# A planned attention and feed-forward kernel: TensorE's order is made to count changes between row-tiled and whole-array work, and the first phase gets its own banks and buffers

## The chip, the core and the metric

The kernel runs on one core of a Trainium2 chip. A core has TensorE (PE in the profile; PEld is its loading of weights), VectorE (DVE), ScalarE (ACT), GpSimd (POOL) and SyncE (SP), which here only issues the data transfers (DMA). The engines run their own instruction streams in order and wait for each other by semaphores. The metric is the device time of one execution in microseconds (us), as the median of several.

## The reference

Four batches of 12608 tokens with 128 channels go through two attentions with 32 inducing rows, and then through a feed-forward layer of width 1024 with a SoLU activation and a normalization. `mab(I, x)` is called p1 here, `mab(x, h)` is p2.

```python
def mab(q, kv):
    s = scale * (q @ kv.transpose(0, 2, 1))
    s = s - s.max(-1, keepdims=True)
    a = np.exp(s)
    a /= a.sum(-1, keepdims=True) + 1e-09
    return a @ kv
h = mab(I, x)
attn = mab(x, h)
...
h = x @ w_in                      # x is attn, as 50432 rows
h_max = np.max(h, axis=-1, keepdims=True)
e = np.exp(h - h_max)
sm = e / (np.sum(e, axis=-1, keepdims=True) + 1e-09)
solu = h * sm
mu = np.mean(solu, axis=-1, keepdims=True)
var = np.mean((solu - mu) ** 2, axis=-1, keepdims=True)
ln = (solu - mu) / np.sqrt(var + 1e-06) * g_ln
return (ln @ w_out).astype(np.float32)
```

The weights come as 64-bit floats and are rounded to 32 bits on the chip.

## The kernel before

A batch has 99 token tiles of 128 rows (396 tiles in all). Its work falls into parts, each written as a generator whose steps (`Op`) name an engine, a cost and what they wait for:

- `p1(b, k)`, nine groups a batch, 12 tiles each (the last has 3 less and a half): x is loaded (line 357), turned by TensorE in three pieces of four transposes (line 561), copied by ScalarE (547), stored to DRAM as xT (571); scores against the inducing rows (589); VectorE takes the maximum (605), TensorE spreads it over the partitions (`fold`, 614), ScalarE exponentiates (637, 639), VectorE turns the weights (659), TensorE gathers (665), VectorE accumulates (681).
- `combine(b)`: the sums and the pooled rows of the batch are brought together (707, 712, 714, the copy of h 716) and multiplied by w_in (726), so that a tile's hidden row is its 32 attention weights times `hs` (copies in 728).
- `p2(b, j)`: xT is read back (753), scores (768), softmax on VectorE, GpSimd and ScalarE (775 to 794), the weights turned by TensorE (804) and copied (812) to `aT`.
- `main` and `soft`, one tile at a time: h = aT times hs (902, products of 32 rows, four of which fit beside each other in the array), VectorE's negative scaling with the minimum (940), ScalarE's exponential (950), GpSimd's product (954), ScalarE's square (965), VectorE's transpose (978).
- `products`, for each four tiles two streams (op0 and op1, each two of the array's four row quarters): 32 steps with w_out (1023), evacuated (1045), finished in `finish` and stored.
- `weights_in`, `weights_out`: load (405), rounding on VectorE (410 to 419), ScalarE (421) and GpSimd (424, 426, 431); for w_out the gains (453), the column means by TensorE (464) and VectorE (469), and 16 transfers that spread it into `wc` (481).

All of this is put in order when the program is built. `Planner` keeps a clock for each engine. At each turn it takes the engine whose next step can begin first, and of that engine's steps that are ready within `SLACK` the one with the lowest priority number. `AFTER` is the time that it reckons between the end of a step on one engine and the start of what depends on it on another. Steps with an `alt` go to whichever engine is free. Where TensorE would stand idle for over `FILL` ns it issues transposes of the identity without use (fillers, line 488). `starts` says at which tile a p1 group, a `combine` or a p2 group is taken up (`P1_FROM`, `P1_STEP`, `P2_START`), `PRIO_P1` and `PRIO_P2` how urgent it is. What the chip does is then this fixed order, with the real waits.

"Row-tiled work" is lines 902 and 1023: matrices of 32 rows, in "beats" of four matmuls that lie side by side and that the profile records as two steps of four. "Whole-array work" is all else on TensorE. In the plan before, a step of whole-array work carries `SWITCH` (170 ns) in its own cost, whatever stands ahead of it.

Batch 0's p1 is the early phase. It borrows space that the later work uses: x goes into parts of `spare` and one of the `xn` buffers (six in all), the weights into the other `xn`; the PSUM banks are those of `op0` and `op1`, and two of a pool that makes room for `h`. `handover` and `handover_op` give them over. w_in is loaded behind the first x.

Of the kernel before, what the change touches and what calls it, by code (L numbers as in the profile page):

```python
# [11 lines left out]
U32 = mybir.dt.uint32  # L12
# [19 lines left out]
EAGER = 60  # L32
SWITCH = 170


def cut(total, most, unit):
# [20 lines left out]
LATE = -13  # L57
ON_EARLY = 3
P1_FROM = 0
P1_GO = 20  # L60
P1_STEP = 8
P2_AHEAD = 29
P2_START = 29
PR_EX = -2
# [5 lines left out]
PR_SQ = 1.5  # L70
PR_TU = 3
# [4 lines left out]
WOUT = -13.5  # L76

AFTER = {
    "PE": {"PE": 0, "ACT": 197, "DVE": 196, "POOL": 200, "SP": 250},
    "ACT": {"PE": 205, "ACT": 143, "DVE": 142, "POOL": 61, "SP": 50},  # L80
    "DVE": {"PE": 256, "ACT": 128, "DVE": 127, "POOL": 155, "SP": 50},
    "POOL": {"PE": 205, "ACT": 75, "DVE": 74, "POOL": 100, "SP": 50},
    "SP": {"PE": 1036, "ACT": 1000, "DVE": 920, "POOL": 1000, "SP": 1000},
# [15 lines left out]
class Op:  # L99
    def __init__(self, eng, cost, fn, *after, prio=None, alt=None, moves=0):  # L100
        self.eng, self.cost, self.fn, self.after, self.prio, self.alt, self.moves = eng, cost, fn, after, prio, alt, moves

# [16 lines left out]
class Planner:  # L119


    def __init__(self, slack):
        self.clock = dict(BEGIN)
        self.ops, self.blocked, self.seq, self.slack = [], 0, 0, slack
        self.window, self.busy, self.slow = 0, {}, True
        self.fill, self.scratch, self.data, self.now = None, (), 0.0, 0.0

# [83 lines left out]

    def run(self):
        clock = self.clock
        while self.ops:
# [3 lines left out]
            pick = min(  # L218
                (o for o in self.ops if o[0].eng == eng and o[1] <= limit),
                key=lambda o: (o[2][1] if o[0].prio is None else o[0].prio, o[3]),  # L220
            )
# [7 lines left out]
            end = start + (self._pe(start, op.cost) if eng == "PE" else op.cost)  # L229
# [9 lines left out]
def set_attention_then_solu_kernel(ctx: ExitStack, tc: tile.TileContext, x, inducing, w_in, w_out, g_ln, out):  # L239
# [51 lines left out]
    op_b = [buf([P, 2, 512], f"op{w}", where=psum) for w in range(2)]  # L291
    op_e = [o[:, i, :] for o in op_b for i in range(2)]
    early_h = tc.tile_pool(name="h_early", bufs=1, space=PSUM, side="right")
    where = early_h.__enter__()
    h_e = [buf([P, 512], f"h_e{i}", where=where) for i in range(2)]
# [16 lines left out]
    OS = Lock(bufs(2, [P, GS, C], "os"))  # L312
# [83 lines left out]
    w_in_ready = Event()  # L396
# [42 lines left out]
    def weights_in():  # L439
        g = yield from rounded(w_in_sb, w_in.bitcast(U32), conv, None, conv_free, -18.5)  # L440
        plan.set(w_in_ready, g)

    def weights_out():
# [11 lines left out]
        o = yield Op("POOL", 200, lambda: nc.gpsimd.memset(wc[:, :, C : C + 1], 1.0))  # L455
        for k in range(KC):
            d = yield Op("ACT", 251, gain(k), g, gd, prio=LATE)
        o_end = [o]
        g = [d]
        mp, rel = yield TRB  # L460
# [13 lines left out]
        give(TRB, mp, d)  # L474
        rows = wc.rearrange("p (k q) d -> p k q d", q=4)
        spread = []
        for a in range(4):
            for q in range(4):
                c = yield dma(
                    M * FF * 4,  # L480
                    lambda: nc.sync.dma_start(rows[a * M : (a + 1) * M, :, q, :C], wg[q * M : (q + 1) * M]), d, issue=600, prio=LATE,
# [30 lines left out]
    EARLY_X = Lock([spare[:, i * each : (i + 1) * each].rearrange("p (s c) -> p s c", c=C) for i in range(SPARES * FF // each)] + xn_b[:1])  # L512
    EARLY_T = Lock([vt_all[:, i * each : (i + 1) * each].rearrange("p (s t) -> p s t", t=P) for i in range(3 * GS * FF // each)] + [xT_b])
    e2 = xn_b[1].rearrange("p s c -> p (s c)")
    EARLY_EW = Lock([(e2[:, i * 2 * PG * M : (i * 2 + 1) * PG * M], e2[:, (i * 2 + 1) * PG * M : (i + 1) * 2 * PG * M].rearrange("p (s m) -> p s m", m=M)) for i in range(2)] + [ew_b])
    EARLY_TR = Lock(op_e[:3])
    EARLY_PB = Lock([*h_e, pb_b, op_e[3]])
# [3 lines left out]
    def p1(b, k):  # L521
# [33 lines left out]
        for c0 in range(0, n, 4):  # L555
# [7 lines left out]
            d = yield Op("PE", SWITCH + 108.7 * (c1 - c0), turn4, [d for d, at in xd if at < c1], trel, prio=None if early else RUSH)  # L563
# [28 lines left out]

        d = yield Op("PE", SWITCH + n * 60, scores, ready, rel, ind_ready.after)

# [19 lines left out]
        d = yield Op("PE", SWITCH + 110, lambda: nc.tensor.matmul(mq, lhsT=fold2, rhs=v["mdiag"], start=True, stop=True), d)  # L614
# [609 lines left out]
```

## Time and profile before

| | us |
|---|---|
| median of 3 runs | 1287.85 (1287.36 to 1296.73) |
| the profiled execution | 1285.68 |
| its span, first to last instruction | 1283.9 |
| TensorE matmuls busy | 1246.2 (97%) |
| TensorE weight loads busy | 1120.8 (87%) |
| VectorE, ScalarE, GpSimd busy | 1140.8, 1140.1, 1104.2 (89, 89, 86%) |
| line 1023 (25600 records) | 1007.7 |
| line 902 (6336 records) | 442.8 |
| mean granted TensorE clock | 0.992 |

Busy times of one engine's groups overlap on TensorE, as matmuls are pipelined and up to four lie beside each other; 1007.7 and 442.8 can't be added. A busy share tells how much of the span has some instruction running, not how well the array is filled. The time by stretch gives the same for parts of the span, with the granted clock and the DMA engines' share; restricted to one line it counts that line's records, so it also tells how far the program is.

### The profile page before, as it was taken

Reading aid. Unit: us, or ns where it says so; the run is one execution under the profiler, and the core shown is the slowest. Engines: PE = TensorE matmul, PEld = TensorE weight load, DVE = VectorE, ACT = ScalarE, POOL = GpSimd, SP = SyncE. Lnnn points to the kernel's source line nnn. Section 1 sums busy time; section 2 is a strip of 40 time slices with the busy share of each in tenths; the row PEclk is TensorE's granted clock in tenths of the full one; section 3 lists DMA queues with packets and bytes.
Section 4 is the critical chain, followed back from the end, with each engine's and each line's share of the span. In section 5 each row is a group of like instructions: output and inputs, shape, how many; then the busy total and the mean of one; then the engine's idle time right before and its main releaser. Section 6 shows DMA issues by size and latency. Waiting matters only on the chain.

```text
span 1283.9 us, 75837 instructions
## 1 busy us (share of the span) xinstructions
PE 1246.2 (97%) x34221; PEld 1120.8 (87%) x34221; DVE 1140.8 (89%) x1825; ACT 1140.1 (89%) x2418; POOL 1104.2 (86%) x981
## 2 busy tenths in 40 slices
PE   8899999999999999999999999999999999999996
PEld 6689888889888888889888998888989999999996
DVE  5589989999898989999888999899999999999993
ACT  5489999999889989999789999989988999999993
POOL 2388988889889988988888997978889999999994
PEclk9999999999999999999899999999999999999998
DMA  9652333331232233332133134233021211111111
GB/s 361 188 164 70 111 103 94 93 111 43 77 117 60 78 102 119 103 109 74 28 102 94 43 103 138 91 101 102 21 82 54 58 55 53 54 38 43 29 29 41
DMA packets 118149, 113.46 MB, mean 88 GB/s; under 512 B 76577, under 2 KB 83777, under 8 KB 117697
## 3 DMA queue, kind: packets, MB, share of 16 engines
q1 hardware_dynamic: 117824, 108.62, 27.6%
q8 instruction: 267, 4.37, 1.4%
q14 instruction: 58, 0.47, 0.1%
HBM read 54.30 MB, written 52.18 MB: 83 GB/s over the span
## 4 chain that ended last, share of the span: by engine, by line
PE 70%; DVE 3%; ACT 2%; issue 1%; POOL 1%; POOLq 0%; DVEq 0%; ACTq 0%
PE op L1023 46%; PE h L902 15%; PE tr L561 2%; PE tr L804 2%; PE tr L768 1%; PE pb L665 1%; PE pb L589 1%; ACT sq L965 1%; DVE spare L940 1%; DVE vt L978 1%; ACT eu L950 1%; POOL eu L954 1%; PE pb L726 0%; DVE hn L940 0%; PE pb L614 0%
## 5 line engine op out<-in xcount | busy, mean ns | idle before, releaser
L1023 PE MATMUL op<-wc,vt 32*128 32x129 f32 x25600 | 1007.7, 275 | 12.5 <-issue 8.4
L1023 PEld LDWEIGHTS op<-wc,vt 32*128 32x128 f32 x25600 | 945.4, 185 | 54.3 <-issue 39.8
L902 PE MATMUL h<-hs,aT 32*128 32x128 f32 x6336 | 442.8, 277 | 3.2 <-DVE spare L940 1.2
L902 PEld LDWEIGHTS h<-hs,aT 32*128 32x128 f32 x6336 | 387.9, 187 | 32.1 <-DVE spare L940 6.2
L954 POOL TENSOR_TENSOR eu<-spare,eu 128x1024 f32<-128x1024 f32 x144 | 341.2, 2376 | 33.8 <-ACT eu L950 33.4
L954 POOL TENSOR_TENSOR eu<-hn,eu 128x1024 f32<-128x1024 f32 x140 | 331.8, 2376 | 25.1 <-ACT eu L950 24.3
L978 DVE STREAM_TRANSPOSE vt<-eu 128x1024 f32<-128x1024 f32 x284 | 349.2, 1233 | 1.1 <-POOL eu L954 0.9
L965 ACT ACTIVATE sq<-eu 128x1024 bf16<-128x1024 f32 x284 | 298.9, 1053 | 17.2 <-POOL eu L954 13.7
L940 DVE TENSOR_SCALAR_CACHE_REDUCE hn<-h,rn 128x1024 f32<-128x1024 f32 x198 | 252.1, 1273 | 38.8 <-PE h L902 30.6
L940 DVE TENSOR_SCALAR_CACHE_REDUCE spare<-h,rn 128x1024 f32<-128x1024 f32 x198 | 251.8, 1272 | 37.2 <-PE h L902 28.2
L950 ACT ACTIVATE eu<-hn,nm 128x1024 f32<-128x1024 f32 x140 | 160.3, 1145 | 19.9 <-DVE hn L940 19.0
L950 ACT ACTIVATE eu<-spare,nm 128x1024 f32<-128x1024 f32 x144 | 164.9, 1145 | 10.7 <-DVE spare L940 10.5
L954 POOL TENSOR_TENSOR spare<-hn,spare 128x1024 f32<-128x1024 f32 x58 | 137.5, 2374 | 15.6 <-ACT spare L950 15.5
L954 POOL TENSOR_TENSOR spare<-spare 128x1024 f32<-128x1024 f32 x54 | 128.0, 2373 | 16.9 <-ACT spare L950 16.4
L978 DVE STREAM_TRANSPOSE vt<-spare 128x1024 f32<-128x1024 f32 x112 | 138.2, 1235 | 0.0
L965 ACT ACTIVATE sq<-spare 128x1024 bf16<-128x1024 f32 x112 | 117.7, 1051 | 9.3 <-POOL spare L954 8.3
L1100 ACT ACTIVATE os<-spare,fin 128x128 f32<-128x128 f32 (+1 forms) x276 | 86.9, 391 | 1.5 <-POOL fin L1085 1.2
L950 ACT ACTIVATE spare<-hn,nm 128x1024 f32<-128x1024 f32 x58 | 66.4, 1145 | 6.7 <-DVE hn L940 6.4
L1045 DVE COPY spare<-op 128x258 f32<-128x258 f32 (+1 forms) x123 | 50.2, 416 | 24.6 <-PE op L1023 23.6
L950 ACT ACTIVATE spare<-spare,nm 128x1024 f32<-128x1024 f32 x54 | 61.9, 1146 | 6.5 <-DVE spare L940 6.5
L965 ACT ACTIVATION_READ_ACCUMULATOR sq<-eu 128x1 f32 x284 | 54.2, 191 | 0.0
L561 PE MATMUL tr<-ident,xn 128*128 128x128 f32 x297 | 48.8, 287 | 0.4 <-DMA xn<-in_x_dram 0.4
(180 smaller groups left out, 1028.0 us busy)
## 6 DMA issues: line engine op xcount, KB each, us to landing
out_dram<-os SPq DMA_DIRECT2D x96, 256.0 KB, 2.4
xT<-xd SPq DMA_DIRECT2D x27, 768.0 KB, 4.6
xn<-in_x_dram SPq DMA_DIRECT2D x22, 768.0 KB, 5.4
xd<-xT SPq DMA_DIRECT2D x21, 768.0 KB, 4.3
dl<-dd SPq DMA_DIRECT2D x396, 1.0 KB, 2.4
xd<-vt SPq DMA_DIRECT2D x7, 768.0 KB, 10.6
spare<-in_x_dram SPq DMA_DIRECT2D x5, 768.0 KB, 10.3
xT<-xd SPq DMA_DIRECT2D x5, 512.0 KB, 4.2
```

What stands on the lines that cost most here:

```text
L561: nc.tensor.transpose(out=tr[:, (s - c0) * P : (s - c0 + 1) * P], in_=xn[:, s, :], identity=ident)
L589: nc.tensor.matmul(sc[g * M : (g + 1) * M, : nn * M], lhsT=indT, rhs=xT[:, :nn, g * M : (g + 1) * M], start=True, stop=True)
L804: nc.tensor.transpose(out=tr[:h, (q - q0) * P : (q - q0 + 1) * P], in_=a4[:, q * P : q * P + h], identity=ident)
L902: nc.tensor.matmul(hp[:, cols], lhsT=aT[rows, i // 2, :], rhs=hs[rows, cols], start=True, stop=True)
L940: lambda: nc.vector.tensor_scalar(out=hn, in0=hp, scalar1=rn, scalar2=None, op0=ALU.mult, op1=ALU.min, accum_out=nm),
L950: "ACT", 1133, lambda: nc.scalar.activation(e, hn, AF.Exp, bias=nm, scale=-1.0, accum_out=G["S"][:, s : s + 1]), d, rel, srel,
L954: d = yield Op("POOL", 2330, lambda: nc.gpsimd.tensor_tensor(out=e, in0=hn, in1=e, op=ALU.mult), de, prio=t + PR_MU)
L965: "ACT", 1040, lambda: nc.scalar.activation(sq, e, AF.Square, scale=1.0 / 32.0, accum_out=G["qe"][:, s, 0:1]), d,
L978: lambda: nc.vector.transpose(out=G["vtb"][:, : n * FF].rearrange("p (j s t) -> p j s t", j=M, s=n)[:, :, s, :], in_=e.rearrange("p (a f) ...
L1023: nc.tensor.matmul(op[:rows, a - 2 * w, : C + 1], lhsT=vt[q, k, :], rhs=wc[q, k, :], start=(k == 0), stop=(k == JB - 1))
L1045: return lambda: eng(F["raw"][:rows, i0 : i0 + 2, :], op[:rows, :, : C + 1])
L1100: nc.scalar.activation(os[:rows, q, :], raw[:, q, :], AF.Copy, scale=y[:, i0 + q : i0 + q + 1])
```

## The change

The plan gets a state for TensorE: `rows` says whether the last step was row-tiled. A change from one to the other costs `SWITCH` (now 200 ns) at that place alone; the steps themselves no longer carry it. `_alike` restricts the choice: as long as row-tiled steps are ready, whole-array steps are held back until two of them (`SEVERAL`) are ready or one has waited 2 us (`PATIENCE`); once in whole-array work, TensorE goes on with it while any is ready. The release times in `AFTER` rise by 40 ns in most pairs, `EAGER` from 60 to 120. A p1 group is taken up every six tiles (`P1_STEP` 8 before), p2's urgency falls (`P2_AHEAD` 29 to 20), other priorities move a little.

In the early phase six PSUM banks of an own pool serve (three for transposes, three beside `pb` for scores), x has nine buffers (two in `wc`, five in `spare`, both `xn`), its weights lie in the `os` buffers. `h`, `op0` and `op1` are made after it. w_in is the first load. `wc` can only be written when the first two groups are done, so its ones (line 455) and the 16 transfers wait for that; the mean uses a bank of the early scores and stands later.

```diff
-EAGER = 60
-SWITCH = 170
+EAGER = 120
+SWITCH = 200
+PATIENCE = 2000
+SEVERAL = 2
...
-LATE = -13
-ON_EARLY = 3
+LATE = -15
...
-P1_STEP = 8
-P2_AHEAD = 29
+P1_STEP = 6
+P2_AHEAD = 20
-PR_EX = -2
+PR_EX = -4
-PR_SQ = 1.5
-PR_TU = 3
+PR_SQ = 2
+PR_TU = 4
+WIN = -20.5
...
-    "PE": {"PE": 0, "ACT": 197, "DVE": 196, "POOL": 200, "SP": 250},
+    "PE": {"PE": 0, "ACT": 237, "DVE": 236, "POOL": 240, "SP": 290},
...
+    def _alike(self, able):
+        rows = [o for o in able if o[0].rows]
+        full = [o for o in able if not o[0].rows]
+        if not rows or not full:
+            return able
+        if not self.rows:
+            return full
+        late = self.clock["PE"] - min(o[1] for o in full) > PATIENCE
+        return full if late or len(full) >= SEVERAL else rows
...
+            able = [o for o in self.ops if o[0].eng == eng and o[1] <= limit]
+            if eng == "PE":
+                able = self._alike(able)
...
-            end = start + (self._pe(start, op.cost) if eng == "PE" else op.cost)
+            cost = op.cost
+            if eng == "PE" and op.rows != self.rows:
+                cost += SWITCH
+                self.rows = op.rows
+            end = start + (self._pe(start, cost) if eng == "PE" else cost)
...
-    op_b = [buf([P, 2, 512], f"op{w}", where=psum) for w in range(2)]
-    h_e = [buf([P, 512], f"h_e{i}", where=where) for i in range(2)]
+    bank_e = [buf([P, 512], f"bank_e{i}", where=where) for i in range(6)]
...
-        mp, rel = yield TRB
+        mp, rel = yield EARLY_PB
...
+        plan.set(centred, d)
+        for k in range(2):
+            yield p1_done[0][k]
+        o = yield Op("POOL", 200, lambda: nc.gpsimd.memset(wc[:, :, C : C + 1], 1.0), [d for e in p1_done[0][:2] for d in e.after])
...
-                    lambda: nc.sync.dma_start(..., wg[q * M : (q + 1) * M]), d, issue=600, prio=LATE,
+                    lambda: nc.sync.dma_start(..., wg[q * M : (q + 1) * M]), d, o, issue=600, prio=LATE,
...
-    EARLY_X = Lock([spare[...] for i in range(SPARES * FF // each)] + xn_b[:1])
+    EARLY_X = Lock([f[...] for f, n in ((wc_flat, 2), (spare, SPARES * FF // each)) for i in range(n)] + xn_b)
-    EARLY_TR = Lock(op_e[:3])
-    EARLY_PB = Lock([*h_e, pb_b, op_e[3]])
+    EARLY_TR = Lock(bank_e[:3])
+    EARLY_PB = Lock([*bank_e[3:], pb_b])
...
-            d = yield Op("PE", SWITCH + 108.7 * (c1 - c0), turn4, [d for d, at in xd if at < c1], trel, prio=None if early else RUSH)
+            d = yield Op("PE", 108.7 * (c1 - c0), turn4, [d for d, at in xd if at < c1], trel, prio=None if early else RUSH)
...
             op.fn = step
+            op.rows = True
...
-        early_h.__exit__(None, None, None)
-        give(H, buf([P, FF], "h", where=pool("h", 1, PSUM, side="right")), *done)
+        bank_pool.__exit__(None, None, None)
+        late = pool("late", 1, PSUM, side="right")
+        give(H, buf([P, FF], "h", where=late), *done)
+        for w in range(2):
+            give(OP[w], buf([P, 2, 512], f"op{w}", where=late), *done)
```

The order is the plan's result. Three places of it follow. First SP at the program's start, that is the transfers in the order in which they are issued (line 357 loads x, 405 a weight, 571 stores xT, 753 reads it back; in the new kernel 375, 423, 593, 775). Before:

```order
L357 DMA spare<-in_x_dram 128x512
L357 DMA spare<-in_x_dram 128x2x512
L498 DMA ind_sb<-in_inducing_dram 32x128
L357 DMA spare<-in_x_dram 128x3x512
L405 DMA eu<-in_moe_w_in_dram 128x2048
L357 DMA spare<-in_x_dram 128x3x512 x3
L357 DMA xn_70<-in_x_dram 128x3x512
L571 DMA xd<-vt 128x1536 x2
L357 DMA spare<-in_x_dram 128x3x512
L571 DMA xd<-vt 128x1536
L405 DMA eu<-in_moe_w_out_dram 128x8x256
L571 DMA xd<-vt 128x1536
```

And now:

```order
L423 DMA eu<-in_moe_w_in_dram 128x2048
L375 DMA wc<-in_x_dram 128x512
L519 DMA ind_sb<-in_inducing_dram 32x128
L375 DMA wc<-in_x_dram 128x2x512
L375 DMA wc<-in_x_dram 128x3x512
L375 DMA spare<-in_x_dram 128x3x512 x5
L375 DMA xn_70<-in_x_dram 128x2x512
L375 DMA xn_71<-in_x_dram 128x512
L375 DMA xn_71<-in_x_dram 128x256
L375 DMA xn_71<-in_x_dram 64x128
L593 DMA xd<-vt 128x1536
L423 DMA eu<-in_moe_w_out_dram 128x8x256
```

Six x loads stood ahead of the first store, and the last groups' loads behind stores and a weight; now w_in stands first, all of x behind it, and the stores behind x.

Next TensorE from the last gather of the early phase to the first tile (line 665 gather, 464 mean, 714 combine, 768 p2's scores, 726 hidden weights, 804 p2's transposes, 902 the tile's product, 488 fillers; in the new kernel 687, 480, 736, 790, 748, 826, 925, 509). Before:

```order
L665 MATMUL h_e_77<-spare,ew 32x128 x7
L464 MATMUL tr<-hn_83,ones_mean 128x128 x8
L714 MATMUL h_e_78<-fold,accn 128x128
L768 MATMUL op_73<-xT_87,h_0_123 32x128 x4
L726 MATMUL pb<-w_in_sb,h_0_123 128x512
L726 MATMUL op_72<-w_in_sb,h_0_123 128x512
L804 MATMUL op_73<-ident,a_94 128x128 x2
L902 MATMUL h<-hs_124,aT_95 128x128 x8
```

And now (729 is the sum of the weights, line 707 before):

```order
L729 MATMUL bank_e_76<-l_134,fold 128x1
L509 MATMUL tr<-ident 128x128 x11
L687 MATMUL bank_e_78<-xn_71,os_104 32x128 x7
L736 MATMUL bank_e_76<-fold,accn 128x128
L748 MATMUL bank_e_79<-w_in_sb,h_0_125 128x512
L748 MATMUL bank_e_80<-w_in_sb,h_0_125 128x512
L790 MATMUL tr<-xT_89,h_0_125 32x128 x4
L480 MATMUL pb<-hn_85,ones_mean 128x128 x8
L509 MATMUL pb<-ident 128x128 x14
L790 MATMUL tr<-xT_89,h_0_125 32x256 x4
L826 MATMUL tr<-ident,a_96 128x128 x2
L925 MATMUL h<-hs_126,aT_97 128x128 x8
```

The mean stood ahead of the combining product and now stands behind the hidden weights and p2's first scores; the hidden weights moved ahead of those scores.

Last TensorE near tile 140, beside p1 of batch 2 (lines as above; 561, now 583, are p1's transposes, 1023, now 1048, the products with w_out). Before:

```order
L1023 MATMUL op_73<-wc,vt 128x129 x2
L561 MATMUL tr<-ident,xn_70 128x128 x4
L1023 MATMUL op_72<-wc,vt 128x129 x2
L1023 MATMUL op_73<-wc,vt 128x129 x2
L1023 MATMUL op_72<-wc,vt 128x129 x2
L1023 MATMUL op_73<-wc,vt 128x129 x2
L1023 MATMUL op_72<-wc,vt 128x129 x2
L1023 MATMUL op_73<-wc,vt 128x129 x2
L665 MATMUL pb<-xn_71,ew 32x128 x12
L1023 MATMUL op_72<-wc,vt 128x129 x2
```

And now:

```order
L1048 MATMUL op_701<-wc,vt 128x129 x2
L1048 MATMUL op_702<-wc,vt 128x129 x2
L583 MATMUL tr<-ident,xn_70 128x128 x4
L687 MATMUL pb<-xn_71,ew 32x128 x12
L583 MATMUL tr<-ident,xn_70 128x128 x4
L925 MATMUL h<-hs_128,aT_99 128x128 x2
L1048 MATMUL op_702<-wc,vt 128x129 x2
```

Transposes and gather stood apart, each between products, and now stand together. Over the whole order whole-array work stands in 237 places between row-tiled work before and in 218 now (after the first tile), and there are 128 fillers before and 178 now.

## Rows read from the trace of the kernel before

**Rows 1.** the page's part 1: engine, busy us, share of the span, instructions.
```profile
PE 1246.2 (97%) x34221; PEld 1120.8 (87%) x34221; DVE 1140.8 (89%) x1825; ACT 1140.1 (89%) x2418; POOL 1104.2 (86%) x981
```

**Rows 2.** time by stretch: length, busy us by engine (records), clock, DMA share, GB/s.
```profile
8.00:40.00 32.00, 29.05 (x368) 20.51 (x369) 24.35 (x78) 19.78 (x45) 9.43 (x10) 1.00 1.02 399
193.00:251.30 58.30, 58.30 (x1590) 50.98 (x1590) 54.71 (x94) 55.04 (x120) 52.04 (x50) 1.00 0.32 102
1006.30:1206.30 200.00, 197.00 (x5862) 185.71 (x5862) 187.86 (x261) 190.04 (x394) 194.01 (x167) 1.00 0.17 45
```

**Rows 3.** time by stretch, line 902 alone (the product h): PE and PEld.
```profile
362.00:608.00 246.00, 87.71 (x1270) 77.39 (x1272) 1.00 0.30 94
610.50:670.80 60.30, 20.92 (x290) 18.35 (x290) 0.94 0.23 67
1006.30:1206.30 200.00, 81.14 (x1152) 69.90 (x1152) 1.00 0.17 45
```

**Rows 4.** time by stretch, line 665 alone (p1's gather).
```profile
362.00:608.00 246.00, 6.68 (x184) 4.53 (x184) 1.00 0.30 94
```

**Rows 5.** timeline of PE at seams: start, length, line, operation, tiles, count.
```profile
83.53 0.85 PE L768 MATMUL tr<-xT,h 128*32 128x384 f32 x8
84.31 0.38 PE L902 MATMUL h<-hs,aT 32*128 32x128 f32 x2
...
91.13 0.85 PE L589 MATMUL pb<-xT,indT 128*32 128x384 f32 x8
91.91 0.66 PE L561 MATMUL tr<-ident,xn 128*128 128x128 f32 x4
92.50 0.83 PE L1023 MATMUL op<-wc,vt 32*128 32x129 f32 x18
...
602.12 2.08 PE L1023 MATMUL op<-wc,vt 32*128 32x129 f32 x68
...
604.80 0.28 PE L902 MATMUL h<-hs,aT 32*128 32x128 f32 x2
605.00 0.64 PE L665 MATMUL pb<-xn,ew 128*32 128x128 f32 x16
605.58 2.29 PE L1023 MATMUL op<-wc,vt 32*128 32x129 f32 x72
```

**Rows 6.** timeline of PE before the first tile.
```profile
39.94 0.53 PE L561 MATMUL op<-ident,spare 128*128 128x128 f32 x3
...
49.10 2.05 PE L464 MATMUL tr<-hn,ones_mean 128*128 128x128 f32 x16
50.99 0.39 PE L714 MATMUL h_e<-fold,accn 128*128 128x128 f32 x2
...
53.09 1.13 PE L726 MATMUL pb<-w_in_sb,h 128*128 128x512 f32 x2
...
56.35 0.38 PE L902 MATMUL h<-hs,aT 32*128 32x128 f32 x2 [0.46 <-ACT aT L812]
```

**Rows 7.** timeline of SP: the issue of the last x loads.
```profile
26.72 2.20 SPq L357 DMA_DIRECT2D spare<-in_x_dram  x3
```

**Rows 8.** timeline of VectorE before the first tile.
```profile
51.26 1.22 DVE L469 TENSOR_TENSOR hn<-tr,hn 128x1024 f32<-128x1024 f32 x1 [1.37 <-PE tr L464]
```

**Rows 9.** timelines of GpSimd and ScalarE: w_out's conversion and gains.
```profile
39.07 2.51 POOL L424 TENSOR_TENSOR hn<-hn,eu 128x512 f32<-128x512 f32 x2 [1.00 <-ACT hn L421]
47.51 2.45 ACT L453 ACTIVATE hn<-hn,g_sb 128x128 f32<-128x128 f32 x8
```

**Rows 10.** timeline of PE at the end of batch 1: the wait for accn.
```profile
635.81 0.79 PE L714 MATMUL pb<-fold,accn 128*128 128x128 f32 x2 [1.92 <-DVE accn L712]
```

**Rows 11.** time by stretch, all engines, at the end of batch 1.
```profile
635.00:640.00 5.00, 4.19 (x66) 3.96 (x70) 3.31 (x5) 2.28 (x4) 2.36 (x2) 0.54 0.03 3
```

**Rows 12.** waits: engine, line, tile, releaser: us in all, times, longest.
```profile
PEld op L1023 <- issue: 39.8, 151, 1.8
PEld h L902 <- DVE spare L940: 6.2, 10, 0.8
```

More of the change, by code (lines that the diff above doesn't have):

```diff
@@ L290, in set_attention_then_solu_kernel @@
     xn_b = bufs(2, [P, PG, C], "xn")
-    op_b = [buf([P, 2, 512], f"op{w}", where=psum) for w in range(2)]
-    op_e = [o[:, i, :] for o in op_b for i in range(2)]
-    early_h = tc.tile_pool(name="h_early", bufs=1, space=PSUM, side="right")
-    where = early_h.__enter__()
-    h_e = [buf([P, 512], f"h_e{i}", where=where) for i in range(2)]
+    bank_pool = tc.tile_pool(name="early", bufs=1, space=PSUM, side="right")
+    where = bank_pool.__enter__()
+    bank_e = [buf([P, 512], f"bank_e{i}", where=where) for i in range(6)]
     tr_b = buf([P, 512], "tr", where=psum)
@@ L439, in weights_in @@
     def weights_in():
-        g = yield from rounded(w_in_sb, w_in.bitcast(U32), conv, None, conv_free, -18.5)
+        g = yield from rounded(w_in_sb, w_in.bitcast(U32), conv, None, conv_free, WIN)
         plan.set(w_in_ready, g)
@@ L591, in scores @@
                 )
-        d = yield Op("PE", SWITCH + n * 60, scores, ready, rel, ind_ready.after)
+        d = yield Op("PE", n * 60, scores, ready, rel, ind_ready.after)
         def free_xT():
@@ L613, in p1 @@
         )
-        d = yield Op("PE", SWITCH + 110, lambda: nc.tensor.matmul(mq, lhsT=fold2, rhs=v["mdiag"], start=True, stop=True), d)
+        d = yield Op("PE", 80 + 110, lambda: nc.tensor.matmul(mq, lhsT=fold2, rhs=v["mdiag"], start=True, stop=True), d)
         first = k == 0
@@ L743, in p2 @@
         A = aT_of[(b, j)]
-        bank = EARLY_TR if b == 0 and j < ON_EARLY else TRB
+        bank = TRB
         prev = []
@@ L1139, in set_attention_then_solu_kernel @@
                 starts.setdefault(NT * (b - 1) + int(P1_FROM + P1_STEP * k), []).append((p1(b, k), PRIO_P1(b, k)))
-        starts.setdefault(max(0, NT * (b - 1)), []).append((combine(b), PRIO_P1(b, NP - 1)))
+        starts.setdefault(max(0, NT * (b - 1)), []).append((combine(b), PRIO_P1(b, NP - 1) if b else -28))
         for j in range(len(at_groups[b])):
@@ L1166, in handover @@
         give(XT, xT_b, *done)
+        for o in os_b:
+            give(OS, o, *done)
         give(EW, ew_b, *done)
@@ L1169, in handover @@
             give(XN, a, *done)
-    def handover_op():
-        done = []
-        for k in range(NP):
-            d = yield p1_done[0][k]
-            done += d
-        for j in range(ON_EARLY):
-            d = yield aT_of[(0, j)]["all"]
-            done += d
-        for w in range(2):
-            give(OP[w], op_b[w], *done)
     def handover_tr():
```

54 lines of the change are left out of this document (29 added, 25 removed).

## The prediction

> **What bounds the kernel now.** I read the engines' totals first, then engine time by stretch, then the timeline wherever TensorE's order has a seam. TensorE's matmul row is busy 97% of 1283.9 us, its weight loads 87%, the other three engines 86 to 89% [rows 1]. A busy matmul row alone is no proof of a bound, so I go by pace. Line 902 leaves 16 records per token tile. From 362 to 608 us, with the next batch's first attention (p1) in the stream, 1270 records are 79.4 tiles in 246 us: 3.10 us a tile. From 1006.3 to 1206.3, with no p1 left, 1152 are 72 tiles in 200 us: 2.78 [rows 3]. The same 246 us hold 184 gather records (line 665), 24 to a full p1 group, so 7.7 groups [rows 4]. Each costs (3.10 - 2.78) x 79.4 / 7.7 = 3.3 us. On TensorE a group is three pieces of transposes at 0.66, scores 0.85, a gather of at least 0.64 and a fold like line 714's 0.39: some 3.9 us by the rows' lengths, of which each of the six pieces overlaps a little with what follows [rows 5, 6]. So p1 is paid nearly in full with TensorE time: beside p1, TensorE is the bound. In the last batch GpSimd is (194.0 of 200 us, against 190.0 on ScalarE and 187.9 on VectorE) [rows 2]; TensorE time saved there buys nothing.
>
> Three places lose more than this pace: the start, whose first tile comes at 56.35 us [rows 6]; the ends of the batches; and the seams where TensorE leaves its 32-row products.
>
> **The early phase.** The last x group sets it. Its transposes end at 40.47 us, since its loads are issued only at 26.72, when a buffer is free; then come fold and gather, the mean matmuls (line 464) from 49.10 to 51.15, the combining matmul (line 714) at 50.99, VectorE's line 469 (1.22 us, queued ahead of the copy of h), the first tile at 56.35 [rows 6 to 8]. The change issues all nine x loads with nothing but a 16 KB load between them, into nine buffers. From 8 to 40 us DMA ran at 399 GB/s [rows 2]; at that rate w_in and x (7.5 MB) are down in some 19 us, and TensorE no longer waits for x. It was busy 29.05 of those 32 us [rows 2], and 22 of the fillers (line 488) stand ahead of the last transposes, at 0.11 us a step: 3.0 + 2.4 = 5.4 us can go. The mean moves behind the hidden weights' matmuls (line 726). That takes some 1.2 us of VectorE (line 469) out of the chain and about 1 of TensorE, but the two line-726 matmuls, 1.13 each, now stand ahead of the first scores: nothing is won by it [rows 6, 8].
> What may hold the start instead is the weights' conversion: GpSimd begins on w_out at 39.07, ScalarE's gains end at 49.96 [rows 9], and in the new order the copies of hs stand behind these gains on ScalarE. The raw w_out can land earlier, with 9.3 MB ahead of and in it, about 23 us at the same rate, but VectorE takes it up between the same p1 groups as now. I take 5.5 us for the phase, between 0 (the gains end where they do) and 9 (TensorE loses all its fillers too).
> Costed at nothing: w_in first puts 1.05 MB, 2.6 us, ahead of the first x. The 32 warm-up transposes cover it; without them it costs those 2.6. The wc spread, 16 issues, follows as one block with the third xT load queued behind it on SP; that load's scores stand ahead of the fifth tile, and if it lands late, up to 3 us are lost (an estimate: one tile's pace; in the bounds).
>
> **The ends of batches.** Counted in TensorE's order, the combining matmul of the next batch stood after 93, 188 and 291 tiles; now it stands after 73, 177 and 276, the batches ending at 99, 198 and 297. The chain combine, hidden weights, p2, first tile gets 21 to 26 tiles of cover instead of 6 to 10. What it cost: at 633 us TensorE waits 1.92 us for accn (VectorE line 712), and the granted clock is 0.54 of 2.4 GHz over the stretch from 635 to 640, its lower level for nearly all of it [rows 10, 11]. Window 610.5 to 670.8: 290 records, 18.1 tiles, in 60.3 us [rows 3]. 18.1 x 2.78 is 50.3; lines 707, 714 and 726 take some 3.0 (0.39, as much again, and twice 1.13); that leaves 7.0, of which the end of a p1 group is at most 3.3. So 3.7 to 7.0 are lost here. I take 5 at this end and 1 for the other two, 6 in all, bounds 0 (the wait moves to tile 177 and stays) and 9.
>
> **Seams on TensorE.** Near 605 us the last pair of 32-row products starts at 604.80, a gather at 605.00, the products resume at 605.58 [rows 5]. A step of products is (2.08 - 0.28)/16 = 0.11 us, so without the gather the next would have begun at 604.91; the gather's own four steps are 0.44. Stopping and starting costs 0.67 - 0.44 = 0.23, and the first step behind it 0.1 more (18 steps in 2.29 us, 17 in 2.08): 0.33 us a round trip. The order has 218 trips instead of 237, and 21 fewer ahead of the last batch. But most merged pairs are of two kinds, a transpose with a gather, and between the kinds the array seems to stop again: scores take 0.78 us to the start of the transposes behind them (91.13 to 91.91), as much as alone to the next product (83.53 to 84.31) [rows 5]. Such a merge saves the entry and the slow step, 0.2. So between 19 x 0.2 = 3.8 and 21 x 0.33 = 6.9; I take 5, near the lower end. Against it, by a count of the order 21 more beats (two steps each, 0.22 us) run with half the array empty, 4.7 us; 4.1 of these lie in the last batch, where GpSimd sets the pace, so 0.6. The 50 additional fillers stand where the plan waits; were there no wait, they would cost 50 x 0.11 = 5.6 us.
>
> **Sum.** -5.5 - 6 - 5 + 0.6 = -15.9 us: the profiled execution, 1285.68 (span 1283.9), goes to 1269.8, and the median of the three runs, 2.2 us higher, to 1272.0.
>
> **Rivals.** (a) TensorE isn't the bound even beside p1, and the seams' time turns into waits: -5.5 - 6, or 1276. For it: ScalarE is busy 55.0 of 58.3 us in a stretch with p1 [rows 2]; against it, the 3.3 us a group. The Trainium skill (Perfetto Trace Analysis, Identifying the Most-Contended Engine) calls matmul busy time a poor measure and goes by the weight loads' share, here 87%; by that the seams give 0 and the time is this rival's.
> (b) The planner's release latencies rise by 40 ns, so instructions are put later where a wait was under-rated, and TensorE's waits for the other engines' buffers shrink. The largest group of these is 6.2 us [rows 12]; two such groups gone give 1259. Against it, far more idle (39.8 us) waits for nothing that the profile names [rows 12], and I see no edit that removes it.
> (c) Slower: p1 every six tiles instead of eight, in some 58 tiles of a batch instead of 87, crowds ScalarE and VectorE there and leaves TensorE idle behind it. If a group then costs 4.0 us while the rest still runs at 2.78, that is 0.7 x 27 = 19 us more: 1291. It cancels the gain from 3.3 + 15.9/27 = 3.9 us a group. For it: ScalarE at 55.0 of 58.3 beside p1 has 6% to give; against it, without p1 it is no less busy, 190.0 of 200 [rows 2], and the pace holds. The Trainium skill (Perfetto Trace Analysis, Optimization Strategy) speaks for this rival: regimes with different bounds gain from interleaving, which a shorter p1 undoes. No run so far shows it.
> (d) The rule hardly acts: seams and half-empty beats cancel, the conversion holds the start (-3), the ends give half (-3): 1282.
>
> **How the numbers follow.** Forecast 0.47, (a) 0.17, (b) 0.12, (c) 0.12, (d) 0.12. About 1% (12.9 us: below 1275, above 1300.7) is what a measurement of this kernel can tell from no change. The forecast, its own range 1264 to 1280, lies below 1275 in three cases of four (0.35), (b) nearly always (0.11), (a) in four of ten (0.07): faster 0.53. Slower takes the far part of (c), with the fillers' 5.6 us and the bounds of the start against me: 0.09. Same: 0.38. The range 1256 to 1289 leaves out the far half of (b), most of (c) and little else, 2 in 10.
>
> **What would show it.** The first tile near 51 us, with x landed by 24; if the gains end after 48, the conversion holds it. No clock dip and no wait for accn near the batches' ends. Some 218 stretches of whole-array work. A pace near 3.25 in the denser stretch and 2.78 behind it; a mean above 3.1 over a batch shows (c). TensorE's waits for VectorE and ScalarE near half: (b). A late third xT load, or pieces held back for a partner that new work waits for, would make the forecast wrong.

## The result and the profile after

The changed kernel takes 1302.05 us (median of 8 runs, 1297.66 to 1303.27) against 1288.22 for the kernel before (8 runs). The ratio is 1.0084, interval 1.0058 to 1.0109: it is slower by 0.6 to 1.1%, where 1272.0 was forecast, and it lies above the stated range (1256 to 1289). The profiled execution took 1297.66 us, its span is 1295.6, 11.7 us more than before's 1283.9.

The engines' totals and time by stretch (columns as in [rows 2]; the last three rows are those of line 925 alone, the old line 902, as in [rows 3]):

```profile
PE 1250.5 (97%) x34271; PEld 1129.3 (87%) x34271; DVE 1142.5 (88%) x1836; ACT 1136.5 (88%) x2410; POOL 1101.9 (85%) x981
```
```profile
8.00:40.00 32.00, 28.82 (x378) 21.13 (x379) 24.33 (x81) 20.21 (x49) 9.97 (x10) 1.00 1.04 400
393.00:398.00 5.00, 4.20 (x87) 4.20 (x90) 2.49 (x4) 4.39 (x11) 4.58 (x10) 0.66 0.08 11
635.00:640.00 5.00, 5.00 (x146) 4.68 (x142) 4.83 (x8) 4.59 (x13) 5.00 (x4) 1.00 0.36 109
1006.30:1206.30 200.00, 197.00 (x5798) 187.00 (x5802) 182.98 (x257) 183.64 (x385) 188.87 (x168) 1.00 0.17 46
...
362.00:608.00 246.00, 88.81 (x1248) 76.49 (x1248) 0.99 0.31 96
610.50:670.80 60.30, 20.91 (x304) 18.48 (x304) 1.00 0.19 48
1006.30:1206.30 200.00, 74.76 (x1082) 65.71 (x1084) 1.00 0.17 46
```

At the end of batch 1 the granted clock is 1.00 where it was 0.54 [rows 11]; a shorter dip now stands near the end of batch 0 (0.66 from 393 to 398 us). The window from 610.5 holds 304 records of h instead of 290. From 1006.3 to 1206.3 there are 1082 records instead of 1152 [rows 3]: the last batch, where the forecast expected nothing, is slower. TensorE is busy the same 197.00 us there, GpSimd 5 us less.

**A ledger of TensorE.** From the start times of all matmul records, between the first and the last 32-row product, I sorted the time by what TensorE was doing. "Trips" is whole-array work with entering and leaving it; "waits" is what a gap has beyond 0.25 us inside the products, 0.30 on entering and 0.34 on leaving:

```
us                        before    after   change   forecast
first tile                  56.4     57.0     +0.6    -5.5
32-row products            982.1    988.3     +6.2    +0.6 (half-empty beats)
trips (237, 218)           203.2    197.3     -5.9    -5.0
waits                       24.7     30.4     +5.7    -6 (ends of batches)
fillers behind tile 1        7.5     12.7     +5.2     0 (5.6 if no wait)
first to last product     1217.5   1228.8    +11.3
```

Next I cut the 31936 product records into 40 equal parts, and took parts 9 and 10, 19 and 20, 28 to 30 as the ends of the batches. The three middles with p1 in them took 722.4 us before and 754.9 after, the three ends 223.1 and 193.0, the stretch behind 139.3 and 138.0, the last eighth 132.8 and 143.0. So the ends gave back 30 us, as p1 and p2 were moved out of them, the middles took 32, and the last eighth lost 10: nearly the whole net loss of 11.3 is there.

Waits of TensorE that the profile names (columns as in [rows 12]), first one more of the kernel before, then after:

```profile
PEld h L902 <- DVE hn L940: 4.0, 7, 0.7
```
```profile
PEld op L1048 <- issue: 30.4, 100, 1.5
PEld h L925 <- DVE hn L965: 17.0, 38, 1.7
PEld h L925 <- DVE spare L965: 10.2, 22, 1.1
```

Idle time ahead of the products with w_out that nothing names fell from 39.8 us [rows 12] to 30.4, but h now waits 27.2 us instead of 10.2 for VectorE to take the h before it out of the one h buffer.

### The profile page after: what moved, and what is told of

It reads as the page before. It is cut to its first block, busy times and chain, and to the rows that moved or that the text cites. A ratio compares the mean times of both kernels' runs of the same rounds, so it can differ in the third digit from the quotient of the medians.

```text
span 1295.6 us, 75921 instructions
## 1 busy us (share of the span) xinstructions
PE 1250.5 (97%) x34271; PEld 1129.3 (87%) x34271; DVE 1142.5 (88%) x1836; ACT 1136.5 (88%) x2410; POOL 1101.9 (85%) x981
## 3 DMA queue, kind: packets, MB, share of 16 engines
q1 hardware_dynamic: 117824, 108.62, 27.2%
## 5 line engine op out<-in xcount | busy, mean ns | idle before, releaser
L1048 PEld LDWEIGHTS op<-wc,vt 32*128 32x128 f32 x25600 | 943.7, 185 | 54.0 <-issue 30.4
L1003 DVE STREAM_TRANSPOSE vt<-eu 128x1024 f32<-128x1024 f32 x284 | 350.3, 1236 | 22.8 <-POOL eu L979 21.9
L979 POOL TENSOR_TENSOR spare<-hn,spare 128x1024 f32<-128x1024 f32 x58 | 137.4, 2371 | 10.7 <-ACT spare L975 10.5
L1003 DVE STREAM_TRANSPOSE vt<-spare 128x1024 f32<-128x1024 f32 x112 | 138.2, 1236 | 9.3 <-POOL spare L979 8.9
L990 ACT ACTIVATE sq<-spare 128x1024 bf16<-128x1024 f32 x112 | 117.8, 1052 | 16.7 <-POOL spare L979 14.9
L1070 DVE COPY spare<-op 128x258 f32<-128x258 f32 x135 | 54.3, 415 | 16.3 <-PE op L1048 14.7
```

What stands on the lines that cost most here:

```text
L979: d = yield Op("POOL", 2330, lambda: nc.gpsimd.tensor_tensor(out=e, in0=hn, in1=e, op=ALU.mult), de, prio=t + PR_MU)
L990: "ACT", 1040, lambda: nc.scalar.activation(sq, e, AF.Square, scale=1.0 / 32.0, accum_out=G["qe"][:, s, 0:1]), d,
L1003: lambda: nc.vector.transpose(out=G["vtb"][:, : n * FF].rearrange("p (j s t) -> p j s t", j=M, s=n)[:, :, s, :], in_=e.rearrange("p (a f) ...
L1048: nc.tensor.matmul(op[:rows, a - 2 * w, : C + 1], lhsT=vt[q, k, :], rhs=wc[q, k, :], start=(k == 0), stop=(k == JB - 1))
L1070: return lambda: eng(F["raw"][:rows, i0 : i0 + 2, :], op[:rows, :, : C + 1])
```

## Experiments

Three counts are read from each kernel's TensorE order: trips to whole-array work behind the first tile, fillers there, and half-empty beats (what the products would take at 0.111 us a step, less what they would take with every step full). Before has 237, 59 and 56.5 us; after 218, 108 and 61.2. The planner is one list scheduler, so a change of any number re-deals the whole order; the counts say how.

### One part of the change taken back

```diff
-            if eng == "PE":
-                able = self._alike(able)
```


> After with the grouping rule off (the planner's choice of TensorE's next piece no longer looks at its mode; the charge of 200 ns for a change stays). Counted in the order: 250 round trips to whole-array work instead of 218, half-empty beats 60.1 us instead of 61.2, fillers behind the first tile 110 instead of 108. Theory T (TensorE is the bound over the whole program, and each trip, half-empty beat and filler in its order is paid): 32 x 0.3 - 1.1 + 0.2 = 8.7 us more than after's 1302.05, 1311. Theory W (the counts are hidden behind other engines, and the loss is of waits that the plan's new numbers make): no change, 1302, within 3.


Measured: 1312.77.

```diff
-EAGER = 120
+EAGER = 60
-    "PE": {"PE": 0, "ACT": 237, "DVE": 236, "POOL": 240, "SP": 290},
+    "PE": {"PE": 0, "ACT": 197, "DVE": 196, "POOL": 200, "SP": 250},
...
```


> After with the release latencies and EAGER of before (40 ns less each, 60 instead of 120). Counted in the order: 204 trips (14 fewer), half-empty beats 81.6 us (20.4 more), fillers behind the first tile 41 (67 fewer, 51 of them in the last tenth of the program). Theory T: 20.4 - 14 x 0.3 - 67 x 0.11 = 8.8 us more than 1302.05, 1311. Theory W: the loss of 10 us in the last eighth goes with the latencies that made the plan late there, 1292.


Measured: 1309.50; the last eighth of the products took 135.6 us instead of after's 143.0, with 0.4 us of waits instead of 5.6.

```diff
-P1_STEP = 6
-P2_AHEAD = 20
+P1_STEP = 8
+P2_AHEAD = 29
```


> After with P1_STEP 8 and P2_AHEAD 29 as before. Counted in the order: 226 trips (8 more), half-empty beats 82.4 us (21.2 more), fillers behind the first tile 200 (92 more, 58 of them in the last eighth). Theory T: 21.2 + 8 x 0.3 + 92 x 0.11 = 33.7 us more, 1336, or 1326 if the fillers lie in real waits. Theory W with the prediction's rival (c), that the dense p1 costs the middles of the batches some 10 us each: the middles come back to before's pace and the ends lose what they had won, 1292 to 1302.


Measured: 1329.73; middles 754.9 again, ends 218.2.

```diff
-PR_EX = -4
-PR_SQ = 2
-PR_TU = 4
+PR_EX = -2
+PR_SQ = 1.5
+PR_TU = 3
```


> After with the softmax's three order numbers of before (PR_EX -2, PR_SQ 1.5, PR_TU 3). Counted in the order: 216 trips, half-empty beats 81.6 us (20.4 more), fillers behind the first tile 125 (17 more). Theory T: 20.4 + 17 x 0.11 - 0.6 = 21.7 us more than 1302.05, 1324. Theory W: the new numbers put ScalarE's exponentials ahead and VectorE's transposes back, and these make GpSimd and the op products wait in the last eighth; without them 1292.


Measured: 1324.88.

All four are slower than after, and each lies within 3 us of theory T's number (for e3, inside its two). Theory W fails for the totals. Only its claim on the last eighth holds, in e2: there the waits went with the latencies and EAGER, but over the whole program 20 us of half-empty beats came in, and these are paid. The ledger of e2 shows it: products 1016.0 us instead of 988.3, waits 21.8 instead of 30.4. Trips cost what was forecast (0.33 us): e1's 32 more cost 11.9 us in the ledger, 0.37 each; after's 19 fewer saved 5.9, 0.31 each.

### Is TensorE the bound in the last batch?

The prediction costed half-empty beats at nothing there.

```diff
+                    if held is None:
...
+                    else:
+                        held.append((p["emit"], 2 * w, p["j"]))
...
+                held = [] if 306 <= t < 378 and t % 3 == 0 else None
-                beats(4, (1 - i % 2,), quarter)
+                beats(4, (1 - i % 2,), quarter, held)
+                for emit, a, k in held or ():
+                    emit(a, k)
+                    emit(a + 1, k)
```


> Before, with the same plan, but in 24 tiles of the last batch (every third from 306 on) the four pairs of h are issued together and the op pairs that went with them behind: both halves of the array are then used one after the other. By the order's count that is 12.3 us more of half-empty steps, all where GpSimd is busy 97%, and h itself is no later. Theory T (TensorE is the bound there too): 12 us over before, 1300. The prediction's step (GpSimd sets the pace there, so half-empty beats cost nothing): no change, 1288, within 3.


Measured: 1298.11, ratio 1.0089 (1.0064 to 1.0113), 10 us of the 12. Time by stretch, all engines, then h alone (line 905):

```profile
1006.30:1206.30 200.00, 196.82 (x5650) 186.31 (x5650) 181.52 (x252) 183.87 (x382) 187.94 (x163) 1.00 0.17 44
...
1006.30:1206.30 200.00, 76.44 (x1110) 67.07 (x1108) 1.00 0.17 44
```

GpSimd, 194.0 us in [rows 2], falls to 187.94 with the slower h (1152 records to 1110): it followed TensorE. Its 97% did not make it the bound: what is added to TensorE's order is paid, at the end too. The Trainium skill (Perfetto Trace Analysis, Identifying the Most-Contended Engine) does not judge TensorE by matmul busy time but by the share of its weight loads, and by its arithmetic against the peak. Over these 200 us that share is 93% in the kernel before (185.71 us, [rows 2]), below GpSimd's 97%, so it pointed away from TensorE; the measurement decides.

### Fillers, and EAGER

```diff
+    shown = []
...
-        nc.tensor.transpose(out=bank[:, :P], in_=ident, identity=ident)
+        shown.append(bank)
+        if len(shown) <= 127:
+            nc.tensor.transpose(out=bank[:, :P], in_=ident, identity=ident)
```


> After, with the same plan, but the 51 fillers that the plan put into the last eighth are not issued; the rest of the order is word for word that of after. If the plan's waits there are not real, each filler costs its 0.11 us: 5.4 us less than after's 1302.05, 1296.6. If they lie in real waits for other engines: no change, 1302, and the rows around their places show TensorE idle instead.


Measured: 1306.29, four more than after rather than five fewer. TensorE's timeline, with the fillers (after) and without:

```profile
1151.51 0.61 PE L925 MATMUL h<-hs,aT 32*128 32x128 f32 x8
1152.05 2.18 PE L509 MATMUL tr<-ident 128*128 128x128 f32 x18
1154.16 1.16 PE L925 MATMUL h<-hs,aT 32*128 32x128 f32 x16
```
```profile
1153.28 0.61 PE L929 MATMUL h<-hs,aT 32*128 32x128 f32 x8
1155.73 1.16 PE L929 MATMUL h<-hs,aT 32*128 32x128 f32 x16 [1.84 <-DVE hn L969]
```
Time by stretch around two of the places, after and then without fillers:
```profile
1140.00:1160.00 20.00, 19.84 (x546) 18.64 (x544) 17.64 (x27) 17.96 (x38) 18.94 (x19) 1.00 0.24 70
...
1260.00:1280.00 20.00, 18.82 (x621) 18.32 (x621) 15.29 (x20) 15.61 (x30) 15.73 (x13) 1.00 0.09 18
```
```profile
1140.00:1160.00 20.00, 18.01 (x480) 16.78 (x476) 17.00 (x26) 17.59 (x37) 18.52 (x20) 0.92 0.24 70
...
1260.00:1280.00 20.00, 17.35 (x425) 16.72 (x426) 16.48 (x23) 17.34 (x35) 17.05 (x11) 0.83 0.10 30
```
Where 2.18 us of fillers stood, TensorE waits 1.84 us for VectorE. The fillers lie in a real wait and cost nothing; without them the granted clock falls (0.92 and 0.83 instead of 1.00). That the 4 us are the clock's is likely, not shown. So the last eighth of after loses some 10 us to waits: 5.4 under fillers, 5.1 more of bare waits than before. At the place shown no op product stands in the wait, and h waits for its own buffer.

```diff
-EAGER = 60
+EAGER = 120
```


> Before with EAGER 120 instead of 60 alone: an op pair may join a beat that starts up to 120 ns, by the plan, ahead of its data. Counted in the order: half-empty beats 50.2 us instead of 56.5, 233 trips instead of 237, the same fillers. Theory T: 6.3 + 4 x 0.3 = 7.5 us less than before's 1288.22, 1281. If the pairs that join early make TensorE wait for VectorE's transposes or for the copies of op, what is won in beats goes there: 1288, with those waits (9.8 us in all at line 1023 for vt, and the copies at 9.9) risen by some 7 us.


Measured: 1289.72, ratio 1.0013 (0.9999 to 1.0027): no gain. The ledger has the products at 982.3 (982.1 before) and waits at 27.6 (24.7). So the beats that are full in the order saved nothing. That a pair joining before its data is there holds the beat is likely, not shown: the waits of TensorE's weight loads for vt and for VectorE's copies of op rose from 3.6 and 4.0 us to 5.7 and 7.2, less than the 7 us in all that were expected.

### Who makes the plan wait: the 40 ns

```diff
-    "PE": {"PE": 0, "ACT": 237, "DVE": 236, "POOL": 240, "SP": 290},
+    "PE": {"PE": 0, "ACT": 197, "DVE": 196, "POOL": 200, "SP": 250},
...
```


> After with the release latencies of before alone (40 ns less each); EAGER stays at 120. Counted in the order: 209 trips (9 fewer), half-empty beats 68.4 us (7.2 more), fillers behind the first tile 41 (67 fewer, none in the last eighth). If the 40 ns make the plan that waits in the last eighth, this eighth (143.0 us in after, 135.6 with both constants back) comes to some 135, and the whole to 1302 - 8 + 7.2 x 1.25 - 9 x 0.33 = 1300. If EAGER makes these waits, the eighth stays at 143 and the whole goes to 1308.


Measured: 1310.67, ten above the count. In the last eighth the waits fell from 5.6 us to 2.1 and the fillers went, so in after the 40 ns made most of the waits there; of the time lost there only half came back (138.2 us, where after has 143.0 and before 132.8). The excess is in the products (1018.9). Part of it goes with the granted clock, which is 0.50 to 0.63 between 70 and 80 us in the profiled execution: of the four executions, two had a mean clock of 0.985 and took 1314.3 and 1313.9 us, two had 0.993 and 0.990 and took 1305.0 and 1307.5. Why the counts miss the rest is open.

Now the 40 ns put into the kernel before, alone (e13), and EAGER alone taken back in after (e14):

> Before with the 40 ns longer release latencies alone (EAGER stays at 60). Counted in the order: 245 trips (8 more), half-empty beats 63.7 us (7.2 more), and 104 fillers in the last quarter where before has none. If the 40 ns alone make the plan wait there: the last quarter of the row products takes 272.1 + 104 x 0.11 = 283 us, and the whole comes to 1287.9 + 11 + 7.2 x 1.25 + 8 x 0.33 = 1311. If they do not, and EAGER 120 or the new order numbers did it in after: the quarter stays at 272 to 274, the whole at 1300.


Measured: 1329.82, ratio 1.0324 (1.0291 to 1.0357), 42 us. The last quarter took 292.6 us instead of 272.1; waits rose to 45.8 us, and not there alone:
```profile
PEld h L902 <- DVE hn L940: 12.0, 19, 1.3
PEld h L902 <- DVE spare L940: 11.3, 15, 1.8
...
PEld op L1023 <- DVE vt L978: 8.6, 19, 1.0
```


> After with EAGER 60 alone (the 40 ns stay). Counted in the order: 217 trips, half-empty beats 78.5 us (17.3 more), 136 fillers behind the first tile (28 more, 61 of them in the last eighth). If the 40 ns make the waits of the last eighth, it stays at 143 us or above, and the whole goes to 1302 + 17.3 x 1.25 = 1324. If EAGER made them, the eighth comes back to 136, and the whole to some 1316.


Measured: 1321.76, the last eighth 141.8. So EAGER 120 is not what slows the last eighth. The 40 ns were expected to spare TensorE waits (rival (b)) and did the opposite, in e13 and in after. How a longer latency in the plan leads to more waiting on the chip was not isolated.

### The other parts alone, on the kernel before

The edits are those of P1_STEP and P2_AHEAD above, and the rule with its charge, put into before.

> Before with P1_STEP 6 and P2_AHEAD 20 alone. Counted in the order: 245 trips (8 more), half-empty beats 66.5 us (10 more), the combining matmuls after 83, 180 and 279 tiles instead of 93, 188 and 291. By the counts: 10 x 1.25 + 8 x 0.33 = 15 us over before, less some 5 us at the end of batch 1 (the wait for accn of 1.92 us and the stretch at the low clock gone): 1298. By the prediction's rival (c) (a p1 group costs 4.0 us instead of 3.3 when p1 is dense, 27 groups) 19 us come on top: 1317. By the prediction's forecast (only the ends change): 1282.


Measured: 1312.91. The ends took 207.2 us instead of 223.1, the middles 760.5 instead of 722.4, so the steps pay 38 for 16. It is neither of the prediction's mechanisms: trips with their work cost 1.0 us more in all; the products took 16.7 more and waits 9.5. The wait for accn only moved: it was 1.92 us near 635 us, and is 1.32 near 319 and 1.43 near 952 here.

> Before with the grouping rule and its charge of 200 ns alone. Counted in the order: 212 trips (25 fewer), half-empty beats 83.0 us (26.5 more), fillers behind the first tile 9 (50 fewer). Theory T: 26.5 x 1.25 - 25 x 0.33 = 25 us over before's 1287.6, 1313 (1308 if the fillers' 5.5 us were paid). The prediction's step (trips saved are won, half-empty beats hardly cost): 25 x 0.33 = 8 us less, 1280.


Measured: 1310.48. Trips fell by 25 and saved 5.0 us in the ledger, the products took 32.6 more. Half-empty beats rose by 26.5 us in the order: held to groups of whole-array pieces, the planner paired fewer products, and that cost more than the trips saved. Within the change it is otherwise: e1, with the rule off, has 60.1 us of them where after has 61.2.

### The early phase

```diff
         hd = yield h_ready[b]
         (s2, mx, nr), srel = yield S2
+        if b == 0 and j:
+            yield aT_of[(0, 0)]["all"]
         sp, rel = yield bank
```


> After, but the attention groups behind the first of the first batch take their transposing bank only once the first group's weights are turned. The read is the first tile alone (the plan behind it comes out otherwise: 17 us more half-empty beats). If the first tile of after is late (56.97) because the second group holds the one bank while its load and its scores are outstanding, ahead of the first group's transposes, it comes at 52.5 to 53.5. If the weights' mean (2.05 us ahead of it) or the hs copies hold it, it stays at 56 to 57.


Measured: first tile 52.69 us (one execution; the whole kernel took 1311.02). TensorE's timeline, after and then this kernel:
```profile
31.23 0.99 PE L583 MATMUL bank_e<-ident,xn 128*128 128x128 f32 x7
...
46.47 0.49 PE L736 MATMUL bank_e<-fold,accn 128*128 128x128 f32 x2 [1.12 <-DVE accn L734]
...
49.67 2.05 PE L480 MATMUL pb<-hn,ones_mean 128*128 128x128 f32 x16
53.11 1.75 PE L509 MATMUL pb<-ident 128*128 128x128 f32 x14 [1.39 <-DVE hn L485]
54.79 0.64 PE L790 MATMUL tr<-xT,h 128*32 128x256 f32 x8
56.09 0.41 PE L826 MATMUL tr<-ident,a 128*128 128x128 f32 x2 [0.66 <-DVE s L797]
56.97 1.16 PE L925 MATMUL h<-hs,aT 32*128 32x128 f32 x16 [0.46 <-ACT aT L834]
```
```profile
49.79 2.05 PE L480 MATMUL pb<-hn,ones_mean 128*128 128x128 f32 x16
51.79 0.44 PE L828 MATMUL tr<-ident,a 128*128 128x128 f32 x2
52.69 1.16 PE L927 MATMUL h<-hs,aT 32*128 32x128 f32 x16 [0.46 <-ACT aT L836]
```
The last transposes of x end at 32.2 us instead of 40.5 [rows 6], and the combining matmul comes 4.5 us earlier. The other 3.8 us were lost behind x. VectorE's timeline in after:
```profile
34.67 1.18 DVE L433 SCALAR_TENSOR_TENSOR eu<-eu 128x1024 uint32<-128x1024 uint32 x1
35.89 1.23 DVE L434 SCALAR_TENSOR_TENSOR eu<-eu 128x1024 uint32<-128x1024 uint32 x1
...
37.89 0.42 DVE L627 TENSOR_REDUCE small<-pb 128x1 f32<-128x256 f32 x1
```
The scores that line 627 takes the maximum of were done at 31.3 us. VectorE comes to them at 37.89, behind the rounding of w_out (five instructions, lines 430 to 437, 4.5 us of the time from 32.72 on), and TensorE runs 26 fillers meanwhile. No run moves the rounding, so what it costs alone is not shown.

Then the first group's transposes, whose input is ready at 51.6, wait 4.5 us: the second group has taken the only transposing bank, and its load, the fillers ahead of it and its scores come first. Before, three groups had banks of their own.

The early phase with that wait, on the planner of before, with three values of EAGER (90 in e12, 60 in e15, 120 in e16):

> Before with the early phase of the change alone (nine x buffers, banks of its own, w_in first, output weights behind the first groups), with the wait that brought the first tile to 52.69 us, and EAGER 90. Counted in the order: 235 trips (2 fewer), half-empty beats 57.2 us (0.7 more), 38 fillers behind the first tile (21 fewer). If what the start wins stays won: 56.35 - 52.7 = 3.7 us less, 1284. If it is lost again behind the start (the early product groups wait for the output weights, or the plan's other order costs as much), 1288, and the time from the first tile to the tenth fortieth of the row products is 4 us longer than before's 326.8.


Measured: 1279.08, ratio 0.9922 (0.9900 to 0.9945), the fastest kernel of this study, and faster than both numbers expected.

> The early phase alone, as in the run before of that kind, but EAGER 60 as in before. Counted in the order: 237 trips, half-empty beats 66.1 us (8.9 more than with EAGER 90), 47 fillers (9 more). If the counts set the time: 1279.1 + 8.9 x 1.25 = 1290. If the gain of that run is the early phase's own: 1280.


Measured: 1288.59, ratio 1.0010 (0.9996 to 1.0024).

> The early phase alone with EAGER 120. Counted in the order: 238 trips (3 more), half-empty beats 54.2 us (3.0 fewer than with EAGER 90). If the counts set the time: 1279.1 - 3.0 x 1.25 + 1 = 1276. If what EAGER saves in beats goes into waits, as it did in before: 1279 to 1282.


Measured: 1293.11, ratio 1.0044 (1.0022 to 1.0066).

The first tile comes at 54.3, 54.0 and 53.9 us in the three, some 2.3 us ahead of before, and the ends differ by 14 us. So at most some 2 us of e12's gain is the early phase's, and with EAGER 60, as in before, nothing of that is left (e15). The rest is the plan that EAGER 90 happens to deal: waits of 18.7 us against 21.9 and 29.3, products 984.1 against 989.8 and 987.4.

### All kernels together

```
          trips  half-empty us  fillers  waits us  median us
before      237       56.5         59      24.7     1288.2
after       218       61.2        108      30.4     1302.1
e1          250       60.1        110      34.1     1312.8
e2          204       81.6         41      21.8     1309.5
e3          226       82.4        200      30.3     1329.7
e4          216       81.6        125      28.5     1324.9
e5          237       68.8         59      26.9     1298.1
e6          215       60.6         57      35.9     1306.3
e7          233       50.2         59      27.6     1289.7
e9          209       68.4         41      25.6     1310.7
e10         245       66.5         61      34.2     1312.9
e11         212       83.0          9      24.4     1310.5
e12         235       57.2         38      18.7     1279.1
e13         245       63.7        132      45.8     1329.8
e14         217       78.5        136      34.6     1321.8
e15         237       66.1         47      21.9     1288.6
e16         238       54.2         38      29.3     1293.1
```
A straight line through these 17 kernels, 1191 + 1.01 x half-empty + 1.62 x waits, leaves 4.2 us (root mean square) of a spread of 14.8. It is fitted, not a test, but these two quantities go with most of the spread. Waits can't be counted in the order; they need a run. The expectations that went by the counts came within 3 us in e1, e2, e4, e5, e11, e14 and e15; in e7, e9, e10, e13 and e16 the kernel was 9 to 19 us slower than they said.

**The parts do not add.** The rule, the steps and the 40 ns each make after slower when they are taken out of it, by 10.7, 27.7 and 8.6 us (e1, e3, e9). Put alone into before, the same three make that slower too, by 22.6, 25.1 and 41.8 us against its runs beside them (e11, e10, e13). So none of them has a price of its own; what one costs alone isn't what it costs within the change.

## Why the prediction was wrong, point by point

- **The bound.** "In the last batch GpSimd is; TensorE time saved there buys nothing" is the first step that failed. e5 shows that TensorE's order is paid there. A share of 97% was taken for a limit because TensorE's own 98.5% (197.00 of 200 us) was set aside. Two terms were put at next to nothing. The products, costed at 0.6 us more, took 6.2 more (4.7 by the count of half-empty beats). The 50 additional fillers, costed at nothing because the plan waits there, mark waits that are real and paid: with the bare waits beside them some 10 us, all in the last eighth.
- **The early phase.** x came as early as costed, and more. The forecast's 5.5 us then fell at a step it did not look at: which piece holds the one transposing bank. The prediction put no price on the banks that the first attention groups lost. It cost 4.3 us (e8): the start gave +0.6, and would have given 3.7 of the 5.5 without it. Ahead of that, 8.3 us of earlier x had shrunk to 4.5 at the combining matmul: VectorE took w_out up between the same groups as before, as forecast, and the last groups' maxima stood behind it.
- **The ends.** The wait for accn and the low clock at the end of batch 1 went, as forecast, and TensorE's waits on entering whole-array work fell by 3.5 us. But those on leaving it rose by 4.8: costed at 6 us less, all waits came to 5.7 more, the largest miss of the sum. The forecast took moved waits for removed ones. Moving p1 and p2 re-deals the order of the middles; done alone this loses 25 us over the whole program (e10), while taking it out of after loses 27.7 (e3).
- **The seams.** Right: 5.9 us against 5, at 0.31 to 0.37 us a trip against 0.33. What grouping can cost elsewhere was mis-sized: alone, in e11, it pays 32.6 us of products for 5.0 of trips; within the change it pays next to nothing (e1).
- **Rival (b)** had the sign wrong. The longer latencies bring waits (e9, e13): after has 5.7 us more in all.
- **Rival (c)** was on the right side with 1291, and the chance of slower was put too low at 0.09. Its mechanism, a p1 group that costs 4.0 us with VectorE and ScalarE crowded, isn't what e10 shows: the products and the waits grew, not the pieces of p1. The Trainium skill (Perfetto Trace Analysis, Optimization Strategy) says that interleaving stretches with different bounds may gain. e10's sign agrees with it, by way of 16.7 us of products and 9.5 of waits; e3's does not, as spreading p1 out again cost after 27.7 us.
- **The sum.** It added four terms as if each edit left the rest of the order alone. By the ledger's rows, of the 27.7 us between the forecast and the profiled execution, waits make 11.7, the first tile 6.1, products 5.6, fillers 5.2, and trips 0.9 the other way. The order's count of half-empty beats was at hand and rose by 4.7 us; it was discounted. Why the middles and the ends came out as they did, part by part, stays open.

## What to carry to other kernels

Where a planner sets the order of an engine that is the bound, count the new order first (steps that run half full, changes of mode, idle slots), price each count from the trace, and discount none of them for another engine's high share unless work added to the first engine is seen to be free. Then run it: the counts see no waits. A constant of a planner is no local edit: three values of one number, with the same early phase, lay 14 us apart. Judge such a kernel by several plans, not by one.

## What was not expected of the hardware

- Adding 12.3 us of steps to TensorE cost 10 us where GpSimd was busy 194.0 of 200 us: GpSimd followed TensorE, and had slack in spite of its share.
- Fillers in a real wait are worth having even late in the program: without 51 of them the granted clock fell to 0.92 and 0.83 in 20 us stretches, and the kernel took 4 us more. In the profiled execution it stands at its lower level (0.50, 1.2 GHz) from 1156.8, 1228.5 and 1262.6 us on for a while, each time soon behind a wait of TensorE: 1.84 us up to 1155.7, 1.49 up to 1227.1, 1.99 up to 1262.4.
